# A four-layer attention kernel on one core: the order of all steps, the engines of its copies and its buffer slots are replaced by another set

## The chip, the core and the metric

The kernel runs on one core of a Trainium2 chip. The core has a matrix engine (PE; its weight loads are listed apart as PEld), a vector engine (DVE), a scalar engine (ACT), GpSimd (POOL) and SyncE (SP), which issues the transfers here. Each engine works through its own list of instructions in order; semaphores make one wait for another. Matmuls write PSUM, which has eight banks of 128 x 2 KB; ACT and DVE read it and write SBUF. The metric is the time of one execution on the device in microseconds. Before the change three runs took 329.66, 329.69 and 329.87 us.

## The reference

One sequence of 2048 tokens, width 512, 32 heads of 16, all bf16. Two kinds of layer alternate (A, B, A, B), each on a layer norm of the running x and added to it:

```
def _A_ref(x, wqkv, w_phi, wo):                      # linear attention
    q, k, v = heads of x @ wqkv
    pq = einsum("bhsd,hdf->bhsf", q, w_phi);  pk likewise from k
    phi_q = concat([softmax(pq), softmax(-pq)]);  phi_k likewise
    kv = einsum("bhsf,bhsd->bhfd", phi_k, v);  z = sum of phi_k over s
    num = einsum("bhqf,bhfd->bhqd", phi_q, kv)
    den = einsum("bhqf,bhf->bhq", phi_q, z) + 1e-6
    return (num / den) @ wo

def _B_ref(x, wqkv, wo):                             # 8 taps, 2 apart
    q, k, v = heads of x @ wqkv
    idx = pos - 2 * arange(8)
    logits = q . k[idx] * 16 ** -0.5, masked where idx < 0
    o = softmax(logits) @ v[idx]
    return o @ wo

x = x + _A_ref(layernorm(x), A_...)
x = x + _B_ref(layernorm(x), B_...)
x = x + _A_ref(layernorm(x), A_...)
x = x + _B_ref(layernorm(x), B_...)
```

## The kernel before

The tokens are cut into four blocks b of 512, each of four tiles t of 128. L = 0, 1 counts the pairs of layers. x stays in SBUF (tiles x0 to x3). The work is written as small steps, each on one engine, in threads named by stage and engine:

- **loads** (`s_loads`, `s_load_B`, all on SP): x by tile or block, the raw query and key weights of A by halves (`wraw`, L327), its value weights (`WA`, L321), the output weights (`WoA`, L331) and B's weights (`WB`, `WoB`).
- **constants and warm-up** (`s_consts`): masks made on DVE from an identity that POOL writes; `kvT` is set to zero (L242), and 14 matmuls of zeros (`warm`, L287) read it.
- **fold** (`s_fold`): w_phi is multiplied into the query and key weights. Per kind 2 x 8 transposes on PE (L364), two copies of 128 x 1024 out of PSUM (`wT`), 4 x 4 products with PHI (L374) and four copies into `WA`. fold0 is the query's, fold1 the key's.
- **layer norm** (`s_ln_first`, `s_norm`): statistics on DVE, one Ln and one Exp on ACT (`lnv`, `rstd`), the normalised `xn` (on ACT, L446, or DVE, L444), and its transpose `xnT`, by PE and a copy or by a DMA (L451).
- **a1** (`s_a1`): per tile the key product (L593) and the value product (L605), two exponentials `Ek` on ACT (L599), the value copy `vaug`; per block (per half in block 3) a tree of sums on DVE, the reciprocal on ACT (L645, L646), one product on DVE (L651) and the sums kv on PE (L668) into one bank over all blocks.
- **a2** (`s_a2`): four query products (L698), eight exponentials `Eq` on ACT (L706), their sums on PE (L714) and two ACT steps (`rS`, L720, L721).
- **akv** (`s_akv`): after the last block's kv, the bank is copied to `kvT`, transposed by PE (L744) and masked on DVE (`ZM`, `R`).
- **a3** (`s_a3`): denominators on PE (L782), DVE (L790, L793), ACT (L796, L797), `rho` on DVE (L801). rho goes to all rows either by PE (L808) with 8 products per block on DVE (L816), blocks 0 and 1, or through DRAM (`Prho`, L831) with two products (L835), blocks 2 and 3. Each of the 8 products reads the PSUM bank directly (*direct*) or a copy of it that ACT makes first (`bs`, L846).
- **a4** (`s_a4`, `s_out`): numerators on PE (L900), copies `oT`, the output product (L520), the residual, squares on ACT (L540) and the next layer norm. The residual is either added on DVE (L533) or by one more matmul with the identity (L523) and copied by ACT (L530).
- **b1** (`s_b1`): twelve products of four matmuls (L927) give QT, K and V with three copies each kind of four; POOL moves 16 columns between blocks; SP spreads V into `Vg` by 16 transfers per block (`vrep`, L988; 4 for each dl = 0 to 3).
- **b2, b3** (`s_b2`, `s_b3`): four products QT x K on DVE (`prod`, L1019), sums on PE (L1026), exponentials and the normaliser on ACT, `PT` on DVE; four products PT x Vg on DVE (`pav`, L1081; the last one in two halves in blocks 2 and 3 of L = 1), sums on PE (L1090), copies, and the output as in a4. Product q = 0 to 3 reads what dl = q brought.

What decides the order is a text: `_ORDER` lists all 1452 steps by a number in base 36 that stands for a thread; each entry takes the next step of its thread. Since every engine works in order, the text fixes each engine's queue, the SP queue of transfers too. `_CHOICE` has one character for each copy, normalised tile and residual that may go on either engine (for residuals 1 means PE with ACT, for bs steps 1 means direct), and `_SLOTS` names, for each tile made, which of 8 PSUM banks (`ps`), 8 large (`big`), 16 middle (`med`) or 6 small (`t2`) buffers it takes. The semaphores follow from reads and writes of these.

```
    def flex(self, stage, fn, *args):
        k = self.nflex
        self.nflex += 1
        self.step(stage, "F%d%s" % (k, fn.__name__), fn, *args, _CHOICE[k] == "1")
...
        for w in _ORDER.split():
            key = self.names[int(w, 36)]
            i = n.get(key, 0)
            n[key] = i + 1
            self.threads[key][i]()
```

Of the kernel before, what the change touches and what calls it, by code (L numbers as in the profile page):

```python
# [57 lines left out]
av 8 i i i i i i i i i i i i 0 f 0 g e 2t 0 bs 9 h a d c 0 j k t i i j l 27 o p 3 3 d6 b 1x 1x t 1y o m 2 2 1q  # L58
1z 1x 1x q u t r 1q v x w n s 1r w 1s 4 20 y 21 1x 22 1x 23 1q 1q 1q 1q 1v 1w z 3d 3d 3d 1u 1t 25 3e 3e 3e z 5
3e 3e z z 26 10 18 18 d5 1 z 16 11 4i 15 6 1h 13 3d 3e 3e 25 25 26 18 25 18 12 26 26 28 26 26 26 26 19 12 28  # L60
2a 28 1h 18 14 12 12 1a 28 1c 3e 2g 2g 1f 2h 2h 1h 1h 1b 1i 2b 1b 1e 1d 29 2j 2k 1h 1j 1n 2r 1b 1l 2s 1b 2c 2r
1k 2s 17 2g 2g 2h 2h 1k 1k 2h 2h 2h 2h 2d 1g 2d 2d 2d 2e 2j 1m 35 36 32 2o 2o 33 2s 33 32 33 33 2r 2s 2s 1o 2o
2o 2d 2r 3a 1k 3a 1p 2p 2o 24 24 2s 24 2u 2v 35 37 2u 2u 2u 2s 2i 2w 2j 3a 2s 3a 2l 2z 2j 24 32 32 34 2m 3b 33
3d 3f 3f 2z 2z 2z 33 2f 33 33 2f 2f 2f 3a 3a 2q 2q 2q 30 3a 2n 3a 3a 2z 3e 2q 2x 35 35 b6 3b 3a 2y 31 31 31 31
3c 3c 38 3c 39 3c 3m 3f 3n 3o 3o 3o 24 24 3g 3g 3g 3f 3p 3q 3g 3g 3g 3g 3g 3r 3q 3f 3g 24 3h 3i 3i 5l 5m 5n 3p
3s 3q 3j 3k 3k 3t 3q 3p 3x 5m 3w 3u 3h 3i 3i 3q 3v 3q 3q 3y 3h 3i 3q 3i 3h 3i 3q 5l 5o 5p 5r 5m 5q 7 7 3z 3q
3i 3j 3k 5m 5l 5s 3k 7 7 5m 5m 5m 3h 3i 7g 40 5u 44 41 42 5t 5m 5m 3j 3j 7h 7i 3k 5v 5m 5w 43 7h 45 7j 45 60
3k 3k 3k 46 45 45 5y 5x 5z 61 61 48 47 47 61 49 47 4a 47 4b 62 47 4b 63 3j 4g 94 4c 45 4d 45 4e 4f 3k 45 45 61
64 63 4h 4p 65 95 7j 7j 66 4q 63 96 95 97 97 63 67 7h 63 67 69 7h 6b 4k 4k 4k 4l 4p 4r 4k 4m 4p 4p 4s 4t 7k 7n
6a 68 6c 4o 7m 50 50 4u 4u 4u 4n 4u 7l 4w 97 7o 7p 7p 7q 7s 3l 4x 7r 7r 7p 7t 7p 6o 7u 50 7r 7r 7v 6o 6j 4v 4y  # L70
4j 6o 6q 6o 4j 4z 6k 6p 6r 6j 7r 6e 6l 95 6d 95 7v 6t 6s 6f 6d 7w 6e 7z 7x 98 9b 9a 99 6g 7y 9c 6e 6j 6j 9d 9d
6u 9d 6e 6n 80 6m 9d 6h 6v 6v 9e 9h 9f 6i 9g 9f 6w 6v 6v 6w 6w 9f 9i 9f 87 88 8h 9j 9f 50 82 9j 9l 6w 6x 6x 87
87 6w 81 83 9n 6x 9k 87 8b 89 51 51 51 51 52 52 8c 8c 8e 6u 6u 6u 9m 8j 8a 8d 8c 6v 6y 3l 8f 82 9o 82 85 82 50
51 52 4z 4z 4z 9q 9q 9s 8c 6z 8g 6y 6z 9r 71 70 6y 6y 6z 6z 72 86 a0 a0 a1 73 84 8i 74 75 74 74 50 74 8i 76 8i
77 a2 76 79 53 53 54 55 54 a5 56 53 54 9v 78 76 9q 9q 76 a0 81 53 9v 9w 9p 7a 57 9v 9u a7 76 7a 9t 8j 7c 9y 54
58 59 59 59 9v 59 9x 7d 7e 5a 8j 8j 7b 7f 5c 5b 5d 5b 5b a0 8k 5e 5b 5f 8k 9z a7 5b 5f 5j 8k 8k 8l a3 5i b4 a4
b7 5h b4 b4 b4 8l 5g b5 b5 a7 b5 b5 a7 8k 8l 8j c3 8i c3 b8 c4 c4 c4 c4 a8 8m a8 a8 a8 c3 a9 a9 5k at c1 b5 a6
8m au au c1 c2 b5 c2 aw c2 c2 a8 a9 b5 b5 8n 8o 8n 8p 8m at au at at 8n 8q 8m a7 aa 8n aw 8r 8s au au au 8s 8s
8t au au 8s 8v a6 a6 8u aa 8w aa 8x 8u 8u 8u 8y ab ac ab ad a6 aa b7 8u b9 b7 c3 8y 90 92 c1 91 c1 c2 8z c2 c2
# [14 lines left out]
if if ig dw ff ig if ig fg fj dw e0 dw ff fg fk ie fl fm fl fn gu fl fl fp ih ih ih ih e1 ii ii ii ik ij fq dy  # L94
# [10 lines left out]
)  # L105


_SLOTS = {
    "big": (
        "0123456701231231456204632073205712053720457604356704213560421356720415763215063506432506"  # L110
    ),
    "med": (
        "0123456789abcdef5837ae98eeaeae471853bc9e43cbe47199ce3185413cebf94c8f74e3581bc71931bc7f370bf9ac21584e"
        "af9c37214a0b589dec37"
    ),
# [1702 lines left out]
```

## Time and profile before

| | before |
|---|---|
| time, median of 3 runs | 329.69 us |
| span of the profiled execution, first to last instruction | 327.5 us |
| granted PE clock over the span | 0.998 |
| PE, DVE, ACT, POOL busy | 310.3, 302.2, 279.3, 25.3 us |
| first transposes of the fold on PE (L364) | 6.41 us |
| transposes of kvT for L = 0 and L = 1 end | 53.6 and 209.2 us |
| last Vg transfer issued | 307.9 us |
| last residual ends | 322.9 us |

The time of the runs is longer than the span by some 2.2 us, which lie before the first and after the last instruction. A row of the groups reads: line, engine, operation, written tile <- read tiles, shape, count | busy us, mean ns of one | idle time before them and what ended it. A row of the order in time reads: start, length, engine, line, operation, count, and in brackets the idle time before it and what ended it.

### The profile page before, as it was taken

The numbers are of one execution on the slowest core, as the hardware profiler recorded it, in microseconds if no ns is written. First come the engines' busy times: TensorE is split into PE (matmuls) and PEld (weight loads), VectorE is DVE, ScalarE is ACT, GpSimd is POOL, SyncE is SP. The second block draws the span as 40 slices with busy tenths as digits, with TensorE's granted clock in tenths as the row PEclk, the third lists the DMA queues.
The fourth block names the chain that finished last, engine by engine and source line by source line (L and its number), as shares of the span: only waits on it lengthen the run. The fifth ranks groups of instructions, "written<-read, shape, count | busy, mean of one in ns | idle before, by whom it ended". The sixth has DMA issues, their size and how long they took to land. (4 is left out here: it accounts for less than half of the span.)

```text
span 327.5 us, 8033 instructions
## 1 busy us (share of the span) xinstructions
PE 310.3 (95%) x3176; PEld 149.5 (46%) x3203; DVE 302.2 (92%) x439; ACT 279.3 (85%) x634; POOL 25.3 (8%) x50
## 2 busy tenths in 40 slices
PE   7999999999999999999999999979999999999873
PEld 3655456445444444443444455644544454433221
DVE  7998995998998999899999999699999999999993
ACT  5999988998888999989999999798999996676550
POOL 4000000000021003000000000000000208400000
PEclk9999999999999999999999999999999999999999
DMA  7980000004556899998750300023436977679952
GB/s 197 380 197 3 0 2 4 2 20 120 105 148 135 152 164 133 139 121 154 137 135 1 67 3 2 4 59 90 128 58 125 179 146 134 150 139 158 166 176 92
DMA packets 37388, 35.41 MB, mean 108 GB/s; under 512 B 23008, under 2 KB 32224, under 8 KB 37344
## 3 DMA queue, kind: packets, MB, share of 16 engines
q1 hardware_dynamic: 36816, 34.81, 53.6%
q8 instruction: 27, 0.44, 0.6%
q14 instruction: 17, 0.14, 0.2%
q10 hardware_dynamic: 528, 0.02, 0.1%
HBM read 10.50 MB, written 2.36 MB: 39 GB/s over the span
## 5 line engine op out<-in xcount | busy, mean ns | idle before, releaser
L927 PE MATMUL ps<-xnT,WB 128*128 128x512 bf16 x384 | 87.6, 380 | 0.5 <-DMA xnT<-xn 0.5
L1081 DVE TENSOR_TENSOR pav<-PT,Vg 128x4096 bf16<-128x4096 bf16 (+1 forms) x34 | 72.0, 2162 | 1.5 <-DMA Vg<-V 1.0
L1019 DVE TENSOR_TENSOR prod<-QT,K 128x4096 bf16<-128x4096 bf16 x32 | 72.5, 2291 | 0.3 <-ACT QT L192 0.2
L927 PEld LDWEIGHTS <-WB 128*128 128x128 bf16 x384 | 42.3, 114 | 43.3 <-issue 5.8
L520 PEld LDWEIGHTS <-oT 128*128 128x128 bf16 x256 | 23.8, 97 | 34.5 <-ACT oT L192 5.7
L192 ACT CAST oT<-ps 128x512 bf16<-128x512 f32 (+1 forms) x60 | 32.1, 587 | 8.4 <-PE ps L1090 7.1
L706 ACT ACTIVATE Eq<-ps 128x512 bf16<-128x512 f32 x64 | 34.0, 615 | 0.7 <-PE ps L698 0.6
L520 PE MATMUL ps<-WoB,oT 128*128 128x512 bf16 x122 | 32.1, 380 | 2.4 <-ACT oT L192 2.0
L599 ACT ACTIVATE Ek<-ps 128x512 bf16<-128x512 f32 x64 | 33.6, 622 | 0.4 <-PE ps L593 0.2
L698 PE MATMUL ps<-xnT,WA 128*128 128x512 bf16 x128 | 30.7, 380 | 0.6 <-DVE Eq L816 0.6
L540 ACT ACTIVATE sqd<-x 128x512 bf16<-128x512 bf16 x48 | 30.1, 643 | 1.0 <-DVE x L533 0.8
L605 PE MATMUL ps<-WA,xnT 128*128 128x512 bf16 x120 | 30.0, 380 | 0.5 <-issue 0.2
L593 PE MATMUL ps<-WA,xnT 128*128 128x512 bf16 x124 | 29.7, 380 | 0.6 <-DMA xnT<-xn 0.2
L520 PE MATMUL ps<-WoA,oT 128*128 128x512 bf16 x120 | 29.2, 380 | 0.4
L533 DVE SCALAR_TENSOR_TENSOR x<-ps,x 128x512 bf16<-128x512 f32 x38 | 25.4, 686 | 1.9 <-PE ps L520 1.7
L192 ACT CAST V<-ps 128x512 bf16<-128x512 f32 x31 | 17.5, 595 | 4.4 <-PE ps L927 4.3
L192 ACT CAST K<-ps 128x512 bf16<-128x512 f32 x31 | 17.8, 585 | 3.7 <-PE ps L927 3.3
L530 ACT ACTIVATE x<-ps 128x512 bf16<-128x512 f32 x26 | 15.1, 598 | 6.4 <-PE ps L523 6.3
L192 ACT CAST QT<-ps 128x512 bf16<-128x512 f32 x29 | 17.1, 592 | 2.5 <-PE ps L927 2.5
L651 DVE TENSOR_TENSOR Ek<-Ek,rk 128x4096 bf16<-128x4096 bf16 (+1 forms) x10 | 18.6, 1858 | 0.5 <-ACT rk L646 0.5
L593 PEld LDWEIGHTS <-xnT 128*128 128x128 bf16 x128 | 12.1, 97 | 15.4 <-DMA xnT<-xn 0.7
L446 ACT ACTIVATE xn<-x,nmr,rstd 128x512 bf16<-128x512 bf16 x23 | 18.2, 822 | 1.0 <-DVE nmr L435 0.8
(129 smaller groups left out, 433.3 us busy)
## 6 DMA issues: line engine op xcount, KB each, us to landing
Vg<-V SPq DMA_DIRECT2D x128, 131.5 KB, 4.4
Prho<-rd SPq DMA_DIRECT2D x8, 512.0 KB
x<-in_A_x_dram SPq DMA_DIRECT2D x3, 512.0 KB
WB<-in_B_wqkv_dram SPq DMA_DIRECT2D x3, 512.0 KB, 11.6
wraw<-in_A_wqkv_dram SPq DMA_DIRECT2D x4, 256.0 KB, 4.5
out_dram<-x SPq DMA_DIRECT2D x4, 256.0 KB, 2.2
out_dram<-x SPq DMA_DIRECT2D x8, 128.0 KB, 2.2
x<-in_A_x_dram SPq DMA_DIRECT2D x4, 128.0 KB
```

What stands on the lines that cost most here:

```text
L192: self.nc.scalar.copy(out=out, in_=in_)
L520: nc.tensor.matmul(y[:], lhsT=oT[:, c, t * P:(t + 1) * P], rhs=Wo()[:, c, :], start=(c == 0), stop=(c == NB - 1 and not onpe))
L533: nc.vector.scalar_tensor_tensor(out=xb[:, t, :], in0=T[t][:], scalar=1.0, in1=xb[:, t, :], op0=ALU.mult, op1=ALU.add, **kw)
L540: nc.scalar.activation(out=sqd[:], in_=xb[:, t, :], func=ACT.Square, accum_out=T["ss"][:, t:t + 1])
L593: nc.tensor.matmul(pk[:], lhsT=xnT[:, t, k, :], rhs=self.WA[:, k, D:2 * D], start=(k == 0), stop=(k == NB - 1))
L599: nc.scalar.activation(out=T["E"][:, t, s, :], in_=T["k", t][:], func=ACT.Exp, scale=1.0 - 2.0 * s)
L605: nc.tensor.matmul(pv[:], lhsT=xnT[:, t, k, :], rhs=self.WA[:, k, 2 * D:3 * D], start=(k == 0), stop=(k == NB - 1))
L698: nc.tensor.matmul(pq[:], lhsT=self.WA[:, k, hb * P:(hb + 1) * P], rhs=xnT[:, :, k, :], start=(k == 0), stop=(k == NB - 1))
L706: nc.scalar.activation(out=self.Eq[L, b][s][:, :, hb, :], in_=T[hb][:].rearrange("p (t i) -> p t i", t=4), func=ACT.Exp, scale=1.0 - 2.0 * s)
L927: nc.tensor.matmul(pp[:], lhsT=self.WB[:, k, i * D + c:(i + 1) * D:NB], rhs=xnT[:, :, k, :], start=(k == 0), stop=(k == NB - 1))
L1019: nc.vector.tensor_tensor(out=pr[:], in0=QT[:, c:c + 1, :].to_broadcast([P, NW, TB]), in1=win, op=ALU.mult)
L1081: nc.vector.tensor_tensor(out=pv, in0=PT[:, :, lo:lo + n].unsqueeze(1).to_broadcast([P, NB, 2, n]), in1=vw, op=ALU.mult)
```

## The change

No step is added or taken away; the three tables are replaced by others. The diff, cut to its first lines:

```
 _ORDER = """
-av 8 i i i i i i i i i i i i 0 f 0 g e 2t 0 bs 9 h a d c 0 j k t i i j l 27 o p 3 3 d6 b 1x 1x t 1y o m 2 2 1q
...
+a 2i 0 0 d6 c d 8 i i i i i 9 i i i i i i i i i 3 1x j k o j p l m b 3 1x 1y o q r 1z 1x 1x 0 1x 0 s t t u 20 21
...
 _CHOICE = (
-    "0011111111111001110111111010000010010000000000000001011111101100100000110101000110000010000001110111"
...
+    "1010111111101111010110111010000001000000001000000100001111111101000000110101000001000110000011110101"
...
 _SLOTS = {
...
     "ps": (
-        "0123456701234750613250746132074365462150743510635127035164051362731405263710452763210743562107423251"
...
+        "0012302450235012342530142657213570623470516234562701530741541372013210456723470152643705167241670314"
```

What the tables say, read out:

| operation | engine | before | after |
|---|---|---|---|
| xn of a tile | DVE / ACT | 41 / 23 | 47 / 17 |
| residual of a tile | DVE / PE and ACT | 38 / 26 | 35 / 29 |
| product with rho, direct / from bs | DVE | 25 / 7 | 22 / 10 |
| QT copies | DVE / ACT | 3 / 29 | 0 / 32 |
| K copies | DVE / ACT | 1 / 31 | 2 / 30 |
| V copies | DVE / ACT | 1 / 31 | 2 / 30 |
| oT copies, 128 x 512 | DVE / ACT | 6 / 56 | 10 / 52 |
| vaug copies | DVE / ACT | 6 / 26 | 5 / 27 |
| kvT copies | DVE / ACT | 1 / 1 | 0 / 2 |
| wT copies | DVE / ACT | 2 / 2 | 1 / 3 |
| xnT copies of one tile | DVE / ACT | 1 / 1 | 0 / 2 |

The head of the queues:

| queue | before | after |
|---|---|---|
| DVE | kvT zero, indAV, indB, indQK, small constants, indDen, maskH, mask2, indS, statistics of x0 ... | maskH, indS (memset and 4 copies), mask2, kvT zero, small constants, statistics of x0 ... |
| SP | x0 (4 tiles), wraw of the query (2), of the key (2), x1, x2, WA, x3, WB (3), WoB (4), WoA (4) | x0 (2), wraw of the query (2), x0 (2), wraw of the key (2), x1, x3, WoA (2), WA, x2, WB (2), WoA, WB, WoB (4), WoA |
| PE | 14 warm, fold0 transposes (16), xn, fold1 transposes (8), fold0 products ... | 14 warm, fold0 transposes (8), xn, fold0 transposes (8), xn, fold0 products (12), fold1 transposes (16) ... |
| ACT | ..., wT of fold0 (first), xnT, wT of fold1 (first), 7 WA copies, Eq ... | ..., wT of fold0 (both), xnT, Ln and Exp, WA copy, wT of fold1 (first), xnT, 6 WA copies, Eq ... |

Further on, among others: the first L = 0 query products and exponentials of block 1 and the sums rS of block 0 change places with the reciprocal of block 3; in L = 1 the sums of a2 of blocks 0 and 1 (L714) stand next to the transposes of kvT instead of some 28 us of PE work earlier; in B of L = 1 the last value products of blocks 0, 2 and 3 stand 5.2, 8.0 and 6.4 us of PE work later in PE's queue; and SP issues the transposes (L451) of blocks 1 and 2 of that layer before the first Vg transfers, not between them.

114 lines of the change are left out of this document (57 added, 57 removed).

## The prediction

> **What bounds the kernel now.** I read the busy shares first, then ten-microsecond windows, then the order in time of the head, the groups of equal instructions, and the list of transfers. The shares are of a span of 327.5 us; the three timed runs have a median of 329.69, so 2.2 us lie around the span. I make every sum on the span's times and add its difference to 329.69.
>
> ```profile
> PE 310.3 (95%) x3176; PEld 149.5 (46%) x3203; DVE 302.2 (92%) x439; ACT 279.3 (85%) x634; POOL 25.3 (8%) x50
> ```
>
> ```profile
> 0.00:10.00 10.00, 8.29 (x66) 4.78 (x67) 8.20 (x32) 6.00 (x12) 3.97 (x27) 1.00 0.79 229
> 10.00:20.00 10.00, 9.95 (x76) 5.64 (x75) 9.38 (x24) 9.84 (x22) 0.38 (x1) 1.00 1.10 342
> ...
> 30.00:40.00 10.00, 9.95 (x56) 4.86 (x56) 9.35 (x13) 9.94 (x21) 0.00 (x0) 1.00 0.00 0
> ...
> 50.00:60.00 10.00, 9.66 (x281) 5.82 (x280) 6.61 (x15) 9.08 (x21) 0.00 (x0) 1.00 0.02 3
> ...
> 200.00:210.00 10.00, 9.54 (x243) 5.82 (x246) 7.86 (x12) 8.68 (x20) 0.00 (x0) 1.00 0.02 3
> ```
>
> The columns are PE, PEld, DVE, ACT, POOL, the granted clock, the DMA share and GB/s. No engine has the whole span. From 10 to 40 us ACT and PE are both full, so what reaches ACT late there stays late. Around 50 and 200 us, where a normaliser chain goes ACT, PE, DVE, ACT, PE, DVE, VectorE idles 3.4 and 2.1 us. From 240 to 317 us VectorE is full but for 0.8 us (the windows from 240 to 290 sum to 49.2 busy). The head:
>
> ```profile
> 0.94 0.27 DVE L242 MEMSET kvT<- 128x256 uint32 x1 [0.94 <-PEq L1802]
> ...
> 1.27 5.30 PE L287 MATMUL ps<-kvT 128*128 128x512 bf16 x14 [1.27 <-DVE kvT L242]
> ...
> 7.06 1.01 ACT L192 COPY wT<-ps 128x1024 bf16<-128x1024 bf16 x1
> ...
> 7.83 0.69 DVE L190 COPY wT<-ps 128x1024 bf16<-128x1024 bf16 x1
> ...
> 13.50 2.60 ACT L706 ACTIVATE Eq<-ps 128x512 bf16<-128x512 f32 x5
> ...
> 47.68 0.31 ACT L645 ACTIVATE s<-s 128x128 f32<-128x128 f32 x1
> ...
> 49.42 0.42 ACT L646 ACTIVATE rk<-s 128x256 bf16<-128x256 f32 x1 [1.43 <-DVE Ek L651]
> ...
> 52.44 0.69 DVE L190 CAST kvT<-ps 128x512 bf16<-128x512 f32 x1 [0.74 <-PE ps L668]
> ```
>
> The 14 warm-up matmuls wait for the memset of kvT and end at 6.57; PE goes straight on to the transposes of the fold (L364), so they end the wait there, not the weights. The two wT copies run side by side on ACT and VectorE.
>
> **The change, part by part.** First the engines, counted over both programs:
>
> ```profile
> L816 DVE TENSOR_TENSOR Eq<-ps,Eq 128x512 bf16<-128x512 f32 x25 | 16.1, 682 | 0.1
> L444 DVE TENSOR_SCALAR xn<-x,rstd,nmr 128x512 bf16<-128x512 bf16 x41 | 14.9, 408 | 0.4
> L816 DVE TENSOR_TENSOR Eq<-bs,Eq 128x512 bf16<-128x512 bf16 x7 | 2.9, 416 | 0.0
> ...
> L446 ACT ACTIVATE xn<-x,nmr,rstd 128x512 bf16<-128x512 bf16 x23 | 18.2, 822 | 1.0 <-DVE nmr L435 0.8
> ...
> L846 ACT CAST bs<-ps 128x512 bf16<-128x512 f32 x7 | 4.1, 589 | 0.0
> ```
>
> VectorE: 6 more xn (+2.45 at 408 ns); 3 fewer residuals, 4 of those with a sum going (686 and 83) and one without coming (-2.39); 3 products from 682 to 416 (-0.80); PSUM copies net +1 at 686 (+0.69); one wT and one half xnT less (688, 418: -1.11). Sum -1.16. ACT: 6 fewer xn (-4.93 at 822), residuals +4 with their sums and -1 without (598 and 204: +2.61), 3 more bs (+1.77 at 589), wT +1 (1.01), half xnT +1 (0.57), other copies -1 (-0.60). Sum +0.43. PE: 3 more identity matmuls, 0.22 apart on the chain of waits: +0.65. None of this is more than 0.4% of an engine. The rest is order.
>
> Second, **the start**. kvT's memset now stands on VectorE behind maskH, the indS memset, its four copies and mask2. maskH still waits for ident (1.41 in the trace); then 0.27, 0.11, 0.46, 0.16 and the memset's 0.27, less some overlap, end at 2.60 instead of 1.21. The warm-ups go from 1.27 to 2.65, +1.38. Their own length is known from both sides only: the first ten weight loads stand 0.428 apart, and from 5.51, 4.2 us after the start, they go twice as fast. If that comes 4.2 us after the start again, they end at 7.95; if it comes at the same 5.5 us of the span, at 7.0; if all 14 run slow, at 8.65. I take 7.95, +1.4, because it keeps the pattern; the ends are +0.45 and +2.1.
>
> The Trainium skill (TensorE: Matmul & The Clock Gate, "The HAM clock gate (the "warmup" mystery)") says that the clock opens after one whole busy window of about 3.4 us and that the windows run free. The 4.2 us here fit it. By it the window that began near 2.1 is no longer wholly busy, the next closes near 8.9, and all 14 run slow: 0.7 more than I take.
>
> From 7.95 I follow the fold by rows. Eight transposes take 0.45; its two wT copies now both stand on ACT, 1.01 each, so they end at 10.5 where before the pair ended at 8.52. The fold's products start at 10.55 (8.63 before). Then the in-order ACT queue: xnT 0.57, a rstd pair 0.49, a WA copy 0.57, wT 1.01, xnT 0.57, two WA copies, each some 0.03 to 0.06 shorter for overlap (seven WA copies took 3.85), ending at 14.65, when the last quarter of the query weights is there; four more WA copies end at 16.8. The first query exponential goes from 13.50 to 16.8: **+3.3**. Queued behind it are all exponentials of the first layer.
>
> Third, **up to the first kv sum**. ACT was busy 33.65 of the 34.18 us from 13.50 to 47.68, so little can be caught up. The queue to the same point (the second half reciprocal of block 3, L645) has 3 more Eq (0.52 apart, +1.55) and one xnT (1.07) and lacks the rS pair (-0.80): +1.8. So it stands at 52.8 (47.68 before). There before had waited till 49.42 for a product. Behind it ACT has 0.73 for the reciprocal, rS 0.80, a copy 0.55, two Eq 1.04: the kvT copy, now on ACT, is at 55.4 to 55.9, against 52.44: **+3.0**.
>
> Fourth, **what comes back**. The early Eq and one projection (0.86 of PE) no longer stand between the transposes of kvT and the normaliser: rho of block 0 comes +2.4 late instead, and the first direct product, 58.17 before, +1.9. From there to the first residual of that block (70.01) VectorE has 0.9 less work: +1.1. But 2.4 of its saving is now used up of 1.16 in all; what is left behind that point is 1.2 longer (0.94 of that after overlaps, 1.1). So at equal idle time later the end is 1.1 + 1.1 = **+2.2**, and 329.69 + 2.2 = 331.9. The extra PE and ACT work hides in PE's gaps of 290 to 320 us and ACT's; without that cover +0.65. The new slots let banks of PSUM be taken again sooner; the waits of PE for a copy or product to leave a bank, in the list of waits, are 0.7 (L714), 0.6 (L698), 0.5 (L808) and 0.2 (L460), 2.0 in all, so -2.0 if all go and +2.0 if they double; I take 0, as both programs have eight banks for the same matmuls. On SP the weights of the value projection (WA) move behind x3 and two WoA transfers, at least 2.5 us of issues; with their 7.3 us to landing they come near 16 to 17, and L605 first reads them at 18.74, which the head makes later still: nothing. In the second layer two transposes (L451) move ahead of block 0's Vg transfers, whose values come 5.2 us later in PE's queue: ready near 253 instead of 247, the first pav of that block (near 258) is met by a landing 4.4 us behind the fourth issue, 0 to 1 us late; I take 0 and leave 1 to the range.
>
> **The rivals.** *A. Head lag stays*: 331.9, as above. For it: ACT and PE full from 10 to 40.
> *B. It is absorbed.* VectorE idles about 11 us between 60 and 290, most of it around 200 to 220 (2.1 and 1.3). If the new order closes a third, -3.7, the end is 329.69 + 2.2 - 3.7 = 328.2. For it: three fewer direct products over both layers, and a2 work of blocks 0 and 1 of the second layer moved into the gap. Against: ACT gets an Eq and an rS pair between the kvT copy and the normaliser, 1.3 us on the very chain that VectorE waits for.
> *C. The values come too late at the end.* PE work behind the last value projection of block 3, second layer, falls from 26.6 to 20.9 us, of block 2 from 30.1 to 22.7.
>
> ```profile
> 267.41 40.52 SPq L988 DMA_DIRECT2D Vg<-V  x48
> ```
>
> Of these, the last 28 transfers, from 287.05 to 307.93, came 0.75 apart. Now 32 (block 2's first four too) can start only near 291: 24 us, to 315.2, and a landing of 2.8 to 4.4 (its shortest and median): 318.0 to 319.6. The last pair of pav products began at 316.2. That is 1.8 to 3.4 late, on a full VectorE. With 2.0 on top of A: 333.9. It decides once V of block 2 is later than 289. Against: PE may run ahead there, as it idles 14 us after 290.
> *D. Nothing shows*: the lag and the closed gaps cancel, 329.7; or the re-search left the balance of engines as it was, as the counts say.
>
> **How the numbers follow.** A 0.40, B 0.28, C 0.22, D 0.10. Likeliest: 331.9, its own range 331.0 (the warm-ups at +0.45) to 332.6 (at +2.1). The whole range takes in B with half the idle closed (329.69 + 2.2 - 5.5 = 326.4) and C with the later landing (335.3): 326.4 to 335.5. Within 0.2%, 0.66 us, is what a measurement of this kernel can't tell from no change: D and the edges of A and B, 0.12. Faster 0.28, slower 0.60.
>
> **What would show it.** The first L287 matmul at 2.6, the wT copies both on ACT with the second ending past 10, the first Eq past 16, the kvT copy past 55: each alone confirms its step. A first Eq before 14.5 would end A. For C, pav waiting on Vg's DMA for 1 us or more after 300. For B, windows around 200 to 220 with VectorE over 9. I am wrong in sign if the kvT copy is late as said and the span is still under 327.

## The result and the profile after

The kernel after takes 348.13 us (median; 346.04 to 349.31) against 329.69 before: 1.0555 times as long, 95% interval 1.0516 to 1.0594, or +18.4 us where +2.2 was forecast. Its profiled execution has a span of 345.6 us (327.5 before), 347.3 with what lies around it. All spans below are of profiled executions, all times are medians, and each ratio is to runs of the kernel before made beside them on the same chip (329.7 to 330.3 us there).

The busy times of the page of after:

```profile
PE 312.2 (90%) x3177; PEld 151.1 (44%) x3206; DVE 301.8 (87%) x437; ACT 281.6 (81%) x639; POOL 22.6 (7%) x50
```

VectorE works as long as before (301.8 against 302.2 us), so none of the 18.1 us of span is work. The loss is waiting. VectorE's gaps, added up from its rows in order of time for eight stages (L is the pair of layers; us; columns for experiments are explained with them):

| stage ends at | before | after | e1 | e4 | e7 | e13 | e14 |
|---|---|---|---|---|---|---|---|
| copy of the first kv sum | 5.4 | 8.7 | 8.7 | 5.8 | 9.3 | 5.9 | 5.6 |
| first pav of block 0, L = 0 | 6.5 | 6.0 | 6.2 | 6.7 | 6.5 | 6.8 | 6.7 |
| first pav of block 3, L = 0 | 1.5 | 5.3 | 3.2 | 10.4 | 1.6 | 1.5 | 1.5 |
| first denominators (L790), L = 1 | 3.2 | 7.7 | 4.5 | 5.0 | 3.4 | 3.3 | 3.2 |
| first QT x K, L = 1 | 2.4 | 4.9 | 4.2 | 2.4 | 2.7 | 3.3 | 3.4 |
| first pav of block 0, L = 1 | 0.8 | 0.5 | 0.5 | 0.8 | 0.8 | 0.5 | 0.3 |
| first pav of block 2, L = 1 | 0.0 | 5.6 | 5.4 | 0.0 | 0.0 | 5.0 | 3.8 |
| end | 5.5 | 5.1 | 6.0 | 5.7 | 5.8 | 5.9 | 5.1 |
| sum | 25.3 | 43.8 | 38.7 | 36.8 | 30.1 | 32.2 | 29.6 |

After stands still 18.5 us longer, in three places: the head (+3.3), the middle of the first B layer to the start of the second pair (+3.8 and +4.5), and the second pair of layers (+2.5 and +5.6).

**The head**, in order of time in the kernel after:

```profile
2.60 4.73 PE L287 MATMUL ps<-kvT 128*128 128x512 bf16 x14 [2.60 <-DVE tiny_t L239]
8.13 1.93 ACT L192 COPY wT<-ps 128x1024 bf16<-128x1024 bf16 x2 [2.79 <-PE ps L364]
15.72 1.13 ACT L706 ACTIVATE Eq<-ps 128x512 bf16<-128x512 f32 x2
54.94 0.59 ACT L192 CAST kvT<-ps 128x512 bf16<-128x512 f32 x1
```

The first exponential `Eq` starts 2.2 us later than before (13.50), the copy of the first kv sum 2.5 us later (52.44).

**The first B layer.** SP's own queue in order of time, first before, then after:

```profile
119.73 19.91 SPq L988 DMA_DIRECT2D Vg<-V  x24
143.44 2.72 SPq L451 DMA_TRANSPOSE xnT<-xn  x1
146.21 2.61 SPq L988 DMA_DIRECT2D Vg<-V  x4
152.09 2.02 SPq L451 DMA_TRANSPOSE xnT<-xn  x1
156.46 12.82 SPq L988 DMA_DIRECT2D Vg<-V  x16
```

```profile
119.61 11.09 SPq L988 DMA_DIRECT2D Vg<-V  x16
144.51 1.75 SPq L451 DMA_TRANSPOSE xnT<-xn  x1
146.38 9.04 SPq L988 DMA_DIRECT2D Vg<-V  x12
155.67 4.92 SPq L451 DMA_TRANSPOSE xnT<-xn  x1
160.64 16.25 SPq L988 DMA_DIRECT2D Vg<-V  x20
```

Before, the 24 transfers from 119.73 hold twelve of block 2's sixteen, and only then comes the transpose of block 1's input for the next layer. After, that transpose stands ahead of those twelve. Between 130.70 (119.61 + 11.09) and 144.51 SP issues nothing, 13.8 us, although the last part of block 2's V was there at 137.8. SP's list of waits in the kernel after says for whom it stood (wait, us in total, times, longest):

```profile
SPq L451 <- DVE xn L444: 35.9, 4, 13.7
```

The chain that ended last in the kernel after carries it on, with pieces left out (start, length, what):

```profile
143.30 1.07 DVE xn L444 x3
144.51 1.75 SPq L451
...
152.29 4.71 DMA Vg<-V
...
167.65 8.76 DMA Vg<-V
176.60 2.29 DVE pav L1081
...
180.16 3.39 PE ps L605 x8
```

The transpose waits for VectorE's `xn`, the twelve transfers for the transpose, block 3's transfers for all of these, `pav` for the transfers. And behind that `pav` on VectorE's queue stand the residuals of block 2, and PE's next value products (L605) wait for them. These products belong to other blocks and read nothing of block 2; what they can wait for is a PSUM bank that such a residual has still to read. The lists of waits of after show both ends of this, and the tail's part too:

```profile
DVE pav L1081 <- DMA Vg<-V: 10.3, 6, 2.8
PE ps L605 <- DVE x L533: 4.2, 1, 4.2
```

Before, `pav` waited for Vg 1.0 us, once. In the ten-microsecond windows of after (columns as in the prediction) PE, VectorE and ACT all fall at 170:

```profile
130.00:140.00 10.00, 8.21 (x55) 3.66 (x54) 7.31 (x4) 8.92 (x24) 0.47 (x2) 1.00 0.70 90
...
170.00:180.00 10.00, 5.91 (x32) 2.47 (x26) 6.28 (x6) 4.43 (x10) 0.00 (x0) 0.99 1.05 144
180.00:190.00 10.00, 9.84 (x62) 3.97 (x62) 8.93 (x15) 9.17 (x24) 0.00 (x0) 0.84 0.37 66
...
200.00:210.00 10.00, 9.95 (x140) 5.45 (x141) 9.60 (x14) 9.97 (x22) 0.00 (x0) 1.00 0.01 2
210.00:220.00 10.00, 9.77 (x284) 6.22 (x284) 6.83 (x12) 8.47 (x20) 0.00 (x0) 1.00 0.01 3
```

VectorE's lower share from 130 to 140 (8.87 before) has another cause: `pav` of block 0 waits 1.1 and 1.6 us there for transfers that SP issued ahead of its pause.

**The second B layer.** The three waits of `pav` in VectorE's order of time, kernel after:

```profile
278.26 2.29 DVE L1081 TENSOR_TENSOR pav<-PT,Vg 128x4096 bf16<-128x4096 bf16 x1 [2.78 <-DMA Vg<-V]
...
321.77 2.29 DVE L1081 TENSOR_TENSOR pav<-PT,Vg 128x4096 bf16<-128x4096 bf16 x1 [1.05 <-DMA Vg<-V]
...
325.40 10.22 DVE L1081 TENSOR_TENSOR pav<-PT,Vg 128x2048 bf16<-128x2048 bf16 x6 [1.34 <-DMA Vg<-V]
```

These are the third of block 0, and of block 3 the third and the first half of the fourth. V of block 2 is complete at 303.3 (282.7 before), of block 3 at 308.0 (286.4). The last 28 transfers leave SP from 308.05 to 329.1, as before in 21 us (287.05 to 307.93), but 21 us later.

### The profile page after: what moved, and what is told of

It reads as the page before. It is cut to its first block, busy times and chain, and to the rows that moved or that the text cites. A ratio compares the mean times of both kernels' runs of the same rounds, so it can differ in the third digit from the quotient of the medians.

```text
span 345.6 us, 8048 instructions
## 1 busy us (share of the span) xinstructions
PE 312.2 (90%) x3177; PEld 151.1 (44%) x3206; DVE 301.8 (87%) x437; ACT 281.6 (81%) x639; POOL 22.6 (7%) x50
## 4 chain that ended last, share of the span: by engine, by line
PE 57%; DVE 11%; DMA 11%; ACT 9%; SPq 7%; issue 3%; POOL 1%; DVEq 0%; POOLq 0%; ACTq 0%
PE ps L927 15%; PE ps L520 9%; DMA Vg<-V 9%; PE ps L605 7%; PE ps L593 6%; SPq L988 6%; PE ps L698 5%; DVE prod L1019 3%; PE ps L668 2%; PE ps L1026 2%; PE ps L1090 2%; DMA xnT<-xn 2%; DVE pav L1081 2%; PE ps L460 2%; DVE Eq L816 1%
## 5 line engine op out<-in xcount | busy, mean ns | idle before, releaser
L927 PE MATMUL ps<-xnT,WB 128*128 128x512 bf16 x384 | 88.0, 380 | 0.6 <-DMA xnT<-xn 0.2
L1081 DVE TENSOR_TENSOR pav<-PT,Vg 128x4096 bf16<-128x4096 bf16 (+1 forms) x34 | 72.8, 2164 | 13.2 <-DMA Vg<-V 10.3
L927 PEld LDWEIGHTS <-WB 128*128 128x128 bf16 x384 | 42.4, 114 | 43.3 <-issue 7.4
L192 ACT CAST oT<-ps 128x512 bf16<-128x512 f32 (+1 forms) x56 | 30.3, 589 | 11.4 <-PE ps L1090 10.2
L520 PEld LDWEIGHTS <-oT 128*128 128x128 bf16 x256 | 23.8, 98 | 34.5 <-issue 5.6
L605 PE MATMUL ps<-WA,xnT 128*128 128x512 bf16 x122 | 31.5, 394 | 5.0 <-DVE x L533 4.2
L520 PE MATMUL ps<-WoB,oT 128*128 128x512 bf16 x121 | 31.8, 380 | 1.7 <-ACT oT L192 1.2
L520 PE MATMUL ps<-WoA,oT 128*128 128x512 bf16 x121 | 29.9, 379 | 1.7 <-issue 1.0
L593 PE MATMUL ps<-WA,xnT 128*128 128x512 bf16 x123 | 29.6, 379 | 0.2
L1090 PE MATMUL ps<-pav,indAV 128*32 128x512 bf16 (+1 forms) x272 | 17.8, 370 | 7.5 <-DVE pav L1081 7.4
L192 ACT CAST QT<-ps 128x512 bf16<-128x512 f32 x32 | 18.4, 604 | 6.1 <-PE ps L927 6.1
L533 DVE SCALAR_TENSOR_TENSOR x<-ps,x 128x512 bf16<-128x512 f32 x35 | 22.7, 684 | 0.5 <-PE ps L520 0.3
L605 PEld LDWEIGHTS <-xnT 128*128 128x128 bf16 x128 | 12.4, 100 | 20.4 <-issue 6.6
L530 ACT ACTIVATE x<-ps 128x512 bf16<-128x512 f32 x29 | 17.0, 594 | 4.4 <-PE ps L523 3.8
L1026 PE MATMUL ps<-prod,indQK 128*32 128x512 bf16 x256 | 16.4, 381 | 4.2 <-DVE prod L1019 4.2
```

The costliest lines, as they stand in the source:

```text
L192: self.nc.scalar.copy(out=out, in_=in_)
L520: nc.tensor.matmul(y[:], lhsT=oT[:, c, t * P:(t + 1) * P], rhs=Wo()[:, c, :], start=(c == 0), stop=(c == NB - 1 and not onpe))
L593: nc.tensor.matmul(pk[:], lhsT=xnT[:, t, k, :], rhs=self.WA[:, k, D:2 * D], start=(k == 0), stop=(k == NB - 1))
L605: nc.tensor.matmul(pv[:], lhsT=xnT[:, t, k, :], rhs=self.WA[:, k, 2 * D:3 * D], start=(k == 0), stop=(k == NB - 1))
L927: nc.tensor.matmul(pp[:], lhsT=self.WB[:, k, i * D + c:(i + 1) * D:NB], rhs=xnT[:, :, k, :], start=(k == 0), stop=(k == NB - 1))
L1081: nc.vector.tensor_tensor(out=pv, in0=PT[:, :, lo:lo + n].unsqueeze(1).to_broadcast([P, NB, 2, n]), in1=vw, op=ALU.mult)
```

## The experiments

The order is a table, so an edit is written as a line of steps, a minus and a plus; every step that isn't named keeps its place and its engine. "Vg b.g" is group g (dl = g, four transfers) of block b, "T b" the transpose of block b's input for the next layer. Buffers were dealt anew in every run, a few or many (26 tiles of 755 take another one in e1, 29 in e4), and what that alone is worth was not tried apart; e2 and e8, and e3 and e13, are the same orders with other buffers, and differ by 3.0 and 1.3 us. The first question was which stretch of the order holds the loss, and whether SP's queue in the first B layer or the tail holds most of it.

**e1: block 2's transfers back in front (L = 0).**

```
-T 1, Vg 2.0, Vg 2.1, Vg 2.2, T 0, Vg 2.3
+Vg 2.0, Vg 2.1, Vg 2.2, T 1, T 0, Vg 2.3
```

> The changed kernel with one edit on SyncE's queue in layer 0: the first three groups of Vg transfers of block 2 (12 transfers) stand ahead of the transpose of block 1's second-layer input again, as before; their two buffers and those that follow are re-dealt to suit. Theory S (in-order SyncE queue: the transpose waits from 130.7 to 144.5 for its xn, and the transfers behind it, whose values were complete at 137.8, wait with it): Vg of block 2 starts near 138, the last pav of layer 0 starts before 181 instead of 185.6, the time falls by 5 to 8 us to 340 to 343. Theory V (value products come late on TensorE): the wait was not what set the end, and the time stays within 1.5 us of 348.1. Theory H (the head's lag): the same as V.

342.90 us, 1.0412 (1.0352 to 1.0472): 5.2 of the 18.4 us come back by the medians (4.7 by the ratios) with one move on one queue. SP now issues 28 transfers in a row, and both transposes behind them:

```profile
119.55 26.03 SPq L988 DMA_DIRECT2D Vg<-V  x28
145.69 11.06 SPq L451 DMA_TRANSPOSE xnT<-xn  x2
156.80 18.22 SPq L988 DMA_DIRECT2D Vg<-V  x20
```

The table shows the gain in the two stages behind it (5.3 to 3.2, 7.7 to 4.5), and that they are still longer than before.

**e4 and e6: the same move put into the kernel before.** e4 is the reverse of e1 but for T 0, which stands behind all sixteen transfers here and behind twelve in after. e6 lets T 0 pass two of the groups as well, which shortens what it waits behind.

```
 e4
-Vg 2.0, Vg 2.1, Vg 2.2, T 1, Vg 2.3, T 0
+T 1, Vg 2.0, Vg 2.1, Vg 2.2, Vg 2.3, T 0
 e6
+T 1, Vg 2.0, Vg 2.1, T 0, Vg 2.2, Vg 2.3
```

> The kernel before with the one edit of the SyncE queue alone: the first three groups of Vg transfers of block 2, layer 0, stand behind the transpose of block 1's second-layer input (as in the changed kernel). S: the 12 transfers start at 146 instead of 128 and push block 3's to about 159 to 172, +2 to +5 us, 332 to 335. If this edit alone is the whole of layer 0's loss: 338 or more. If it costs nothing by itself: 329.4 to 330.4.

> The kernel of e4 with the transpose of block 0's second-layer input issued behind the first two groups of Vg transfers of block 2 instead of behind all four (so two groups, 8 transfers, move behind it). Theory S1 (e4's 10.9 us come from TensorE standing still for 9.2 us for this transpose, which stood behind transfers): the wait falls to 2 to 5 us and the time to 333 to 337. Theory S2 (they come from the pav products waiting for their Vg): the transfers are later still, and the time stays at 340 or more.

e4: 341.13 us, 1.0335 (1.0313 to 1.0358), **+10.9 us from one transpose on one queue**, twice what e1 gave back and above the range expected for S. e6: 337.62, 1.0239 (1.0198 to 1.0281). In order of time in e4 (SP, PE, VectorE):

```profile
159.14 6.26 SPq L451 DMA_TRANSPOSE xnT<-xn  x1
...
168.12 1.89 PE L593 MATMUL ps<-WA,xnT 128*128 128x512 bf16 x4 [9.16 <-DMA xnT<-xn]
...
175.73 0.69 DVE L1054 TENSOR_TENSOR PT<-E,rden 128x1024 bf16<-128x1024 bf16 x1 [7.26 <-ACT rden L1049]
```

Here the second transpose is the victim. It stands behind the sixteen late transfers, and PE, which works in order, stands 9.16 us for it with the normaliser of block 3 queued behind. VectorE then waits 7.26 us for that normaliser. In this window PE and ACT are almost at rest:

```profile
160.00:170.00 10.00, 1.88 (x5) 0.73 (x6) 5.80 (x3) 0.00 (x0) 0.00 (x0) 0.59 1.12 159
```

In e6 PE's wait for the transpose is gone (0.7 us), and VectorE's gap of that stage falls from 10.4 to 6.8; what is left is `pav` waiting for the groups that still come late (2.57 and 2.07 us in block 2, 1.86 in block 3; the list puts the 2.57 to a PE step, but the four transfers of that `pav` were issued only from 157.0). So the transfers of one block and the transpose behind them are one queue: whichever goes second makes somebody wait.

**e12: block 2's V earlier in L = 0 (rival).** In e1 V of block 2 was complete at 138.0. The rival says that it, and not SP, holds the rest.

```
 PE  -... fourth value product of block 2 in its place of after
     +... next to the third
 SP  -T 1, T 0, Vg 2.3
     +Vg 2.3, T 1, T 0
```

> The kernel of e1 (changed kernel with its SyncE queue of layer 0 mended, 342.9 us) with the last value product of block 2 in layer 0 directly behind its third (values complete near 128.5 instead of 138), and the fourth group of its Vg transfers issued ahead of the transposes too. Theory V: the transfers of block 2 end near 142, block 3's start at 158 instead of 162.9, the last pav of layer 0 at 176 to 178 instead of 181.3, and the time is 337.5 to 340. Rival (buffers or products on VectorE hold block 3): within 1.5 us of 342.9.

342.34, 1.0378 (1.0338 to 1.0417): the intervals of e1 and e12 overlap almost whole. V came at 132.6, 5.4 us earlier, and nothing came of it that the two intervals can show. The rest of this stretch isn't V of block 2.

**e2 and e8: the front of after, the tail of before.** Joined at the first QT x K product of L = 1.

```
 steps up to the first query product of B, L = 1: as in after
-the rest: as in after
+the rest: as in before
```

> The changed kernel up to the first query product of the second B layer (all engines, step 1122 of 1453), and from there the order of before for all steps that are left. Theory V+S (two separate losses, about 9.5 us in layer 0 by the lag of the second layer's kv sum, and about 9 us in the second layer's B stage): only the first is left, 338 to 341, and the values of blocks 2 and 3 are complete near 296. If the second loss is only what the first one sets off, the time stays at 346 to 349. If the loss is all in the tail, it falls to 329 to 332.

> As e2 (changed order up to the first query product of the second B layer, order of before behind), with the buffers dealt anew so that none is waited for where before does not wait: in e2 the second half of a Prho load waited for its buffer until 249.6, and VectorE 5.0 us for it. Front and tail are two separate losses: 338 to 341, being 9.5 us for the front. If it stays at 345 or more, the front also costs in the tail.

e2: 345.97, 1.0485 (1.0419 to 1.0551). It is spoiled by its seam: half a load of `Prho` had to wait for a buffer until 249.6, and VectorE 5.0 us for it. e8 is the same with other buffers: 343.01, 1.0383 (1.0334 to 1.0432). It too has 5.8 us of idle time on VectorE at the seam where before has 2.4, so its +12.7 hold more than what the front costs. If front and tail simply added, the tail of after would cost 5 us or more; the next pair measures it.

**e3 and e13: the front of before, the tail of after.**

```
 steps up to the first query product of B, L = 1: as in before
-the rest: as in before
+the rest: as in after
```

> The reverse: the order of before up to the first key product of the second B layer (step 1115), then the changed order for all steps that are left. V+S: only the second loss, 337 to 341, with the values of block 2 complete at 291 to 298 instead of 282.7, and the last 28 Vg transfers starting there. If the tail's order is harmless by itself: 329 to 332.

> The kernel of e3 (order of before up to the second B layer, changed order behind) with its PSUM banks and buffers dealt anew: in e3 TensorE stood still for 2.0 us at 243.0 for a bank that the changed kernel doesn't wait for there. If the tail's loss is the order's own: 336 to 338, and VectorE still idle for over 4 us between block 0's first pav and block 2's. If it was the dealing: 332 to 334.

e3: 338.0, 1.0243 (1.0218 to 1.0269), with a wait of PE of 2.0 us for a bank at the seam. e13 is without that wait: 336.73, **1.020 (1.0182 to 1.0219), +6.6 us for the tail alone**. With the head of before and no delay in the first B layer, V of block 2 is still complete only at 292.9 in e13 (282.7 before; 294.6 in e3, which holds the wait at the seam), and two copies on POOL follow it:

```profile
292.96 2.38 POOL L969 COPY vh<-V 128x64 bf16<-128x64 bf16 x1 [9.27 <-ACT V L192]
295.40 2.18 POOL L965 COPY V<-vh 128x64 bf16<-128x64 bf16 x1
```

**e7 and e11: the head alone.** e7 takes after's order up to the copy of the first kv sum, then before's. e11 undoes two of its edits.

```
 e7  steps up to the copy of the first kv sum: as in after; the rest: as in before
 e11 from e7
-maskH, indS, mask2, kvT zero
+kvT zero, maskH, indS, mask2
-second wT copy of fold0 on ACT
+second wT copy of fold0 on DVE
```

> The changed order up to the copy of the first kv sum (step 292), the order of before behind it. This is the head alone, of which the prediction made +2.2 us: in the changed kernel's trace the copy stands at 54.9 instead of 52.4. Head lag stays: 331.5 to 332.5. Absorbed: 329.5 to 330.5. Nothing else of the change is in it, so 333 or more would be a third cause.

> The kernel of e7 (changed order up to the first kv sum, 333.0 us) with the two edits of the head's start undone: the memset of kvT first on VectorE, and the second wT copy of the first fold on VectorE instead of ScalarE. The prediction's working: the start makes 3.3 us of lag at the first query exponential, of which ScalarE has 1.8 us more work in any case up to the kv sum. If the start's lag is carried through (theory A): the first query exponential near 14 instead of 16.1 and 331 to 332. If the work put ahead of the kv sum decides instead: 332.5 to 333.5 although the exponential is early.

e7: 333.0, 1.0094 (1.0064 to 1.0124), +3.1 us by the ratio; the median lies 0.5 above the range given for head lag alone, at the value given for a third cause, but the interval reaches into that range. e11: 332.1, 1.007 (1.0043 to 1.0096). The two intervals overlap, so the times alone don't show what the two edits are worth. In the order of time, on ACT and VectorE, the first `Eq` comes 0.9 us earlier in e11 and the copy 1.1. First e7, then e11:

```profile
16.12 1.13 ACT L706 ACTIVATE Eq<-ps 128x512 bf16<-128x512 f32 x2
...
55.52 0.69 DVE L190 CAST kvT<-ps 128x512 bf16<-128x512 f32 x1 [0.64 <-PE ps L668]
```

```profile
15.25 1.13 ACT L706 ACTIVATE Eq<-ps 128x512 bf16<-128x512 f32 x2
...
54.42 0.69 DVE L190 CAST kvT<-ps 128x512 bf16<-128x512 f32 x1 [0.41 <-PE ps L668]
```

One pair of traces isn't enough for that, as executions of one head differ by as much; all twenty together say more. With after's head (after, e1, e2, e7, e8, e12) the first `Eq` starts from 15.72 to 17.02 and the copy from 54.94 to 56.25, 16.3 and 55.6 on average. With before's (twelve traces) they start from 13.45 to 14.63 and from 52.40 to 53.57, 13.9 and 52.8 on average. With the two edits undone, in e11 and e15, `Eq` is at 15.25 and 14.93, the copy at 54.42 and 54.17. So the two edits are worth half of the lag at most, the less as the warm-ups of these two happen to end early (5.80 and 5.86, against 6.5 on average in the twelve). That the rest lies in the order of the steps between is argued, not shown.

**e9 and e14: block 0 in the tail.** In e3's tail the last value product of block 0 comes late, and SP has the transpose for block 2 ahead of block 0's transfers. e9 moves the product alone; e14 (from e13) the product and the transfers.

```
 PE  +fourth value product of block 0 next to its third        (e9, e14)
 SP  -T 1, T 2, Vg 0.0, Vg 0.1
     +T 1, Vg 0.0, Vg 0.1, T 2                                  (e14)
 ACT, POOL  the copies and the halo copy of that product go with it
```

> The kernel of e3 (order of before up to the second B layer, changed order behind) with the last value product of block 0 in the second layer directly behind its third on TensorE, and its copies together on ScalarE. In e3 these values were complete at 254.1 (247.2 before), and VectorE stood still for 2.3 us at 266 to 268.5 for the Vg transfers made from them. Theory V (each late block of values costs its own wait): complete near 249.5, that gap gone, 335 to 336.5 instead of 338.0. Rival (the tail is bound later, by the last 28 transfers, whatever happens at 268): 337.5 to 338.5, with the gap moved behind 300.

> The kernel of e13 with two edits together: block 0's last value product next to its third (as e9), and on SyncE's queue its first two groups of Vg transfers ahead of the transpose for block 2 (before's order), which in e9 held them until 255.3 although their values were complete at 250.5. Theory S+V (late value and queue hide each other, so that neither alone gives anything): the 2.3 us wait of pav for Vg near 268 is gone and the time is 1.5 to 3 us under e13. Rival (the tail is bound by the last transfers): the same as e13 within 1 us.

e9: 340.6, 1.0325 (1.0285 to 1.0366), slower than e3. V of block 0 was complete at 250.5 instead of 254.1, but the transfers stood behind the transpose until 255.4, and VectorE now waits 3.0 us at 252 for the product of a residual (0.5 in e3), since PE does the moved product first (20 matmuls of L927 ahead of L520 in place of 16). e14: 334.76, 1.0138 (1.0119 to 1.0157), 2.0 us better than e13, and the wait of `pav` near 268 is gone. The same pair as in the first B layer: data that is early helps only if the queue that carries it is free.

**e5 and e16: the values of blocks 1 to 3 earlier in the tail.**

```
 PE, ACT, POOL  +last value product of block 1, all of block 2, last of block 3
                 ahead of the projections they stood behind     (e5 from e3, e16 from e14)
 buffers        +those that come free first, for Vg of block 1's second half and block 2   (e16)
```

> The kernel of e3 (order of before up to the second B layer, changed order behind) with one kind of edit: in the second layer the last value product of block 1, all four of block 2 and the last of block 3 go earlier on TensorE, with their copies on ScalarE, and the halo copies on GpSimd between these blocks' values directly behind them. Theory V (the tail's 7.8 us are the lateness of the values: block 2's were complete at 294.6 instead of 282.7, and the last 28 transfers could only start then): values of block 2 complete near 276 to 284, last transfer issued before 315 instead of 319.4, time 331 to 335. Rival (the tail loses by the order of products and residuals on VectorE): 337 to 339, no change from e3.

> The kernel of e14 with the edits of e5 (values of blocks 1, 2 and 3 of the second layer earlier on TensorE) and, at the same time, buffers that are free earlier for the Vg of block 1's second half and block 2's first (in e5 these transfers stood until 290.9 for a buffer that a product held). Theory S+V+buffers: the transfers of block 1 end before 284 instead of 289.6, those of block 3 start at 291 to 294 instead of 296.5, pav's waits for Vg after 300 (3.3 us in e14) fall to under 1 us, and the time is 332 to 333.5. Rival (the order of products and pav on VectorE is the rest of the loss, the transfers only follow it): 334 to 336.5.

e5: 340.15, 1.0321 (1.0275 to 1.0367), slower than e3 although V of block 2 was complete 21 us earlier (273.5): the transfers for block 1's second half waited for a large buffer until 290.9. e16: 335.98, 1.0191 (1.0177 to 1.0204), slower than e14. There the waits of `pav` after 300 are gone altogether, and VectorE waits earlier instead, 2.57 us at 274.3, for PE's sums of products (L1026), which now stand behind the values. But the last transfers are not early: V of block 3 is complete at 290.2 and its transfers start only at 296.1, behind a wait of 13.4 us that the list puts to a QT x K product, so a large buffer was still taken and the edit of the buffers missed its aim. What is moved forward in PE's queue moves something else back.

**e17: where in the tail.** The front of before reaches to the first `pav` of block 0.

```
 steps up to the first pav of block 0, L = 1: as in before; the rest: as in after
```

> The order of before up to the first pav of the second layer's block 0 (step 1225 of 1453), the changed order behind: the part of the tail that e14 mended is before's own, and what is left of the change is the order of block 1's to 3's projections, products and pav. If the rest of the tail's loss (4.8 us in e14) lies in that order: 333.5 to 336. If it is made earlier, between the first query product and the first pav: 329.5 to 331.5.

335.77, 1.0181 (1.015 to 1.0213). Block 0's values and transfers are as in before here, and still +6.0 us are left, behind that point, with `pav` waiting 4.4 us for Vg in four places, from 304 on.

**e20 and e21: block 1 and block 2 brought forward.** Before does block 1's sums, its normaliser and its first two `pav` between the products of block 2; after does all eight products of blocks 2 and 3 first but for one.

```
 from e17
 PE   -sums of block 1's products: 1, then 2, then 1, with projections between
      +all four, then the normaliser; last value product of block 1 next to its third
 DVE  -products of blocks 2 and 3 (seven), pav 1.0, product, pav 1.1, pav 1.2, pav 1.3
      +product, pav 1.0, product, pav 1.1, products of blocks 2 and 3 (six), pav 1.2, pav 1.3   (e20)
 PE, ACT, POOL +value products of block 2 with copies and halo hop ahead of block 3's   (e21)
 SP   +Vg 2.0 ahead of Vg 1.2 and Vg 1.3                                              (e21)
```

> The kernel before up to the first pav of block 0 in the second B layer, behind it the order of after, but with block 1 brought forward as before has it: its sums of QT x K on PE and its normaliser next to each other, its last value product next to its third, and its first two pav on VectorE between the products of block 2 instead of behind all eight products of blocks 2 and 3. The values of blocks 2 and 3 stay late. Theory (the late normaliser and the late pav of block 1 hold the large buffers, and VectorE runs out of anything else at the end): pav's waits for Vg after 300 fall from 4.4 us to under 2, span 331 to 332.5 against 334.7, time 332.5 to 334. Rival (the values of block 2 are too late, whatever VectorE does before): their transfers stay where they are, the waits move by less than 1 us, span 334 to 335, time 335 to 336.5.

> The run with block 1 brought forward, and block 2's four value products on PE with their copies and halo hop brought forward too, ahead of the projections of block 3. Theory that both together make up the tail's loss: no wait of pav for Vg over 1 us, span 329 to 330.5 against 327.5 of the kernel before, time 330.5 to 332. Rival (PE is full there, so that earlier values make the products of block 3 late by as much): span within 1 us of the run with block 1 alone, with VectorE's waits in front of the products of block 3 instead of in front of pav.

Both fell short: e20 339.03, 1.0281 (1.0249 to 1.0314), above both of its ranges; e21 338.68, 1.0267 (1.0236 to 1.0297), some 3 us slower than e17. Block 1's `pav` came at 278 and 282 as meant (290 and 295 in e17). In e20 the waits of `pav` after 300 didn't fall but rose, from 4.4 to 5.9 us; but V of block 2 is complete at 297.6 there, 4.5 us later than in e17. In order of time on VectorE, e20 and then e21:

```profile
306.89 2.29 DVE L1081 TENSOR_TENSOR pav<-PT,Vg 128x4096 bf16<-128x4096 bf16 x1 [2.51 <-DMA Vg<-V]
310.28 2.29 DVE L1081 TENSOR_TENSOR pav<-PT,Vg 128x4096 bf16<-128x4096 bf16 x1 [1.10 <-DMA Vg<-V]
```

```profile
296.73 4.49 DVE L1019 TENSOR_TENSOR prod<-QT,K 128x4096 bf16<-128x4096 bf16 x2 [2.98 <-ACT QT L192]
```

In e21 the largest wait has gone to the products of block 3, whose `QT` copy is late now. V of block 2 is complete at 284.1 there. An earlier normaliser of block 1 alone didn't give the tail back, then, but as e20 also made block 2's values later, the two runs don't part these causes; no single move was found that gives it back.

**e15: all that was found, put into after.** e1, e11's two edits and e14's.

```
 from after: SP of e1; head edits of e11; PE and SP of e14
```

> The changed kernel with every mend of this study that could be tried: SyncE's queue in layer 0 (e1), the head's two edits (e11) and the second layer's values and queue (e14). e1 alone gave 342.9; e11's edits took 0.9 off. Theory: 339 to 341.5. If the gains hide behind one another: 342 to 343. Below 330 it would beat both kernels, which nothing so far suggests.

340.06, 1.0319 (1.0285 to 1.0353): 8.1 of the 18.4 us come back. No kernel of this study is faster than the one before.

## Why the prediction was wrong

The sign was right and the mechanism of the likeliest case was seen; the size was not, 18.4 us against 2.2.

**Engines.** VectorE -1.16 was forecast, -0.4 measured; ACT +0.43 against +2.3; PE +0.65 against +1.9. The prediction said at most 0.4% of an engine; measured it is at most 0.7%, the 2.3 us of ACT, which is five times its sum. It was right that the rest is order.

**The start.** The first L287 matmul came at 2.60, where 2.65 was forecast, and both wT copies stand on ACT, the second ending at 10.06 (10.5). The warm-ups ended at 7.33, not 7.95; the first `Eq` is at 15.72 instead of 16.8, and the copy at 54.94 instead of 55.4 to 55.9, so that two of its signs (`Eq` past 16, the copy past 55) missed narrowly. That is chance as much as error: over the six traces with this head the warm-ups end at 7.33 to 8.64, 7.9 on average, and the forecasts of all three lie within what these traces show. The head alone costs 3.1 us (2.1 to 4.1, e7), and the forecast of +2.2 is inside. This part held.

**The queue of SP in the first B layer: the step that failed.** The prediction followed SP's transposes past Vg at one place, "in the second layer two transposes (L451) move ahead of block 0's Vg transfers", priced it "0 to 1 us late" and took 0. (Only the transpose of block 2 moves there; that of block 1 stood ahead of them before, too.) The same kind of move in the first B layer, T 1 past twelve transfers of block 2, isn't in the sum at all. By e1 it is worth 5.2 us within after, by e4 10.9 us alone in before, where the other transpose stands behind four more transfers. It could have been priced from rows of before: the transpose there starts at 143.44, right when its `xn` is there, so that transfers put behind it start no earlier than 145, and block 2's had started near 128. That is 17 us of delay for a block whose `pav` and residuals the next layer's PE work waits for. The step in the text that rests on it is "so at equal idle time later the end is": VectorE's idle time behind the kv copy went from 19.9 to 35.1 us.

**Rival C, the values too late at the end.** Its mechanism is there: V of block 2 past 289, `pav` waiting for Vg after 300. Mis-sized was its term "1.8 to 3.4 late", taken as 2.0: the tail alone costs 6.6 (e13). Its 291 was right for PE, whose last value product of block 2 ends at 291.3 in e13. But the copy of that product completes V only at 292.9, the first four transfers start at 292.96, and block 3's stand behind two halo copies on POOL until 297.60, so that the last one leaves SP at 318.4 and not at 315.2. With the forecast's own landing of 2.8 to 4.4 that would be 5.0 to 6.6 us late, an estimate; as `pav` waits only 1.3 us for Vg after 300 in e13, it isn't shown that these transfers hold VectorE for all of it. And it took only the last transfers as late, while the longest wait of e13, 2.62 us at 267.8, is one of block 0's. That wait goes, and 2.0 of the 6.6 us with it, when the value product and the transfers of block 0 are moved together (e14), the very move priced at 0. What is left, 4.6 us in e14 and 6.0 in e17, arises behind the first `pav` of block 0 and stays open: values earlier (e5, e16), block 1 earlier (e20) or both (e21) each moved the wait to another place. One thing is common to all thirteen kernels with after's tail: the span ends 15.9 to 17.5 us after the last Vg transfer has left SP, though that happens anywhere from 316.9 to 329.1. So the end and the last transfer move together; which of them sets the other isn't shown, and that the cause is the joint order of PE's projections, sums and values with VectorE's is argued, not shown.

**Rival B, absorbed.** Wrong: the windows 200 to 220 have 9.60 + 6.83 = 16.43 us of VectorE, against 7.86 + 8.69 = 16.55 before; nothing was closed. Its sign, a window over 9, came true in one of the two without that. **Rival D** falls with the time.

**The sum.** Head 3.1, SP's queue 5.2, tail 6.6: 14.9 of 18.4. The three were measured in different kernels, and e1 and e4 show that such parts need not add (5.2 against 10.9 for nearly the same move). The remaining 3.5 wasn't tried apart; the A layer of the second pair has 2.5 us more idle time in the table, of which e13, with the front of before, shows 0.9.

## What to carry to other kernels

Where every engine and every transfer queue works in order, compare the queues that issue transfers step by step through the whole program, in each layer, and price every step that waits by what now stands ready behind it: one transpose moved past twelve transfers cost 5 to 11 us here, while no engine's work grew by more than 2.3. Busy times say nothing of such a change; the idle time of the fullest engine, cut by stage, finds the place at once. And in these runs data made earlier helped only when the queue that carries it had room, so test such moves in pairs.

## What the runs showed of the hardware

How long a DMA transpose holds its issuing queue varies with what went before it. On SP it took 1.75 us where nothing was in flight (after, 144.51), 4.92 behind twelve Vg transfers (after, 155.67) and 6.26 behind sixteen (e4, 159.14). It isn't in proportion to their number, though: 5.17 behind eight (e6, 151.81), and 4.07 behind 28 (e1, 145.69). What in it waits wasn't tried.

The 14 warm-up matmuls start 0.43 us apart at first and 0.22 us apart later, and where that changes differs from one execution to the next, with no change in what is issued. In the fourteen traces in which they start at 1.26 or 1.27 they end between 5.79 (e16) and 7.09 (e6); in the six in which they start at 2.60, between 7.33 (after) and 8.64. So the prediction's "4.2 us again" was not a constant. The Trainium skill (TensorE: Matmul & The Clock Gate, "The HAM clock gate (the "warmup" mystery)") says that the windows run free, and that the same kernel can have 6, 11 or 14 slow matmuls by their phase at its start. The counts here agree: seven are slow in e11, eleven before, all 14 in e12. The spread that the same section gives, 0.5 us around 4 us of activity, is too narrow for these runs: the change comes 2.9 to 5.4 us after the first matmul, and in e12 not within 6.0. The version drawn from the skill in the prediction, that all 14 would run slow and end at 8.65, did not come in the trace of after, but it came in that of e12, at 8.64.

Where PE stood still, the granted clock was lower: 0.59 from 160 to 170 us in e4 with 1.88 us of PE work, and in after 0.84 from 180 to 190, behind a window with 5.91 us.

GpSimd's halo copies of 128x64 take up to ten times as long beside VectorE's large products as without them. In order of time on POOL, and on VectorE, kernel after, second B layer:

```profile
263.98 0.24 POOL L969 COPY vh<-V 128x64 bf16<-128x64 bf16 x1 [4.40 <-ACT V L192]
...
303.41 2.37 POOL L969 COPY vh<-V 128x64 bf16<-128x64 bf16 x1 [9.28 <-ACT V L192]
305.84 2.18 POOL L965 COPY V<-vh 128x64 bf16<-128x64 bf16 x1
```

```profile
303.40 2.28 DVE L1081 TENSOR_TENSOR pav<-PT,Vg 128x4096 bf16<-128x4096 bf16 x1
305.61 2.32 DVE L1019 TENSOR_TENSOR prod<-QT,K 128x4096 bf16<-128x4096 bf16 x1
```

Each long copy ends 0.1 us after the product it ran beside (305.78 after 305.68, 308.02 after 307.93), as if it had waited for that to end; the copy at 263.98 ran beside a residual that reads PSUM. In the other traces, too, such copies take 0.23 to 0.41 us where no such product overlaps them, and most of those that start beside one end 0.1 us after it. The two above take 4.55 of the 4.7 us between V of block 2 (303.35) and the first transfer of block 3 (308.05). The Trainium skill (GPSIMD Engine Reference, "1. Specifications") says that GpSimd shares its SBUF interface with VectorE, with contention where VectorE's instruction has two SBUF inputs; the trace agrees, with 2.37 beside such a product and 0.24 beside the residual. What the end would gain if these two copies stood elsewhere wasn't tried.
